# A hand-ordered attention and mixing kernel: q and k of the last batch transposed by DMA, less bias on TensorE, four loads in flight instead of six, and a new order

## The chip, the cores and the metric

The kernel runs on one core of a Trainium2 chip. The metric is the device time of one execution in microseconds (us). Every execution also gives the mean clock that was granted to TensorE, where 1.0 is full speed. One execution of each kernel was taken with the hardware profiler; the profile's span leaves out some 1.8 us of the device time.

## The reference

Four batches, eight heads, 768 positions and heads of 64. Attention comes first, over a window of 96 positions and 8 global ones. A mixer over tokens and channels follows, batch by batch.

```python
scores = scale * np.matmul(q, k.transpose(0, 1, 3, 2))
bias   = -slopes[:, None, None] * dist[None, :, :]
scores = np.where(keep, scores + bias, -1e9)      # keep: 8 global keys, or 0 <= rel < 96
a = softmax(scores)
x = np.matmul(a, v)                               # as (B, S, H*D)

theta = x @ w_theta
zr, zi = x * np.cos(theta), x * np.sin(theta)
u = x + w_tok_r @ zr + w_tok_i @ zi               # matrices of 768 x 768 over the tokens
out = u + np.maximum(u @ w_ch, 0.0)               # float32
```

## The kernel before

All work is cut into small named operations, and one long list, `ORDER`, fixes the order of the instructions on every engine. **Each engine takes its part of the list in that order**, and an instruction that waits holds what stands behind it: the changed kernel's VectorE, shown below, stood 4.84 us at one copy, with a normalise behind it whose matmuls had ended. The names that matter here are `t` (transposes of q or k), `q` and `k` (their evacuation from PSUM), `kp`/`kg` (a twin copy of transposed k), `bi` (bias matmuls), `s` (scores), `x` (exponential), `m` (multiply by a table), `vpa`/`vpb` (copies of the v tile, `vp<-vn`), `v` (the values matmul), `n` (normalise), `mx` (token mixing) and `ch` (channel mixing). The digits are batch, third of the sequence, pair of heads. `/DVE` and `/ACT` name the engine, and `+3` puts three filler matmuls on zeros ahead of an operation.

The constants, the loads with their gates, and the copies of v:

```python
    TQ = ()                 # thirds whose q and k are transposed by DMA
    DEPTH = 6               # loads in flight, batches 2 and 3
    DEPTH1 = 8              # batch 1
    BIASED = (0, 1, 2)      # thirds of batch 0 whose bias is added on TensorE
...
    def load(fn, us, ndesc, spot, depth=0, reads=(), writes=(), alloc=None):
        nload[0] += 1
        n = nload[0]
        landed[n] = spot
        ...
        if depth:           # the gate: a 1x1 copy out of the load `depth` before this one
            add(f"gate{n}", {"POOL": 0.35},
                lambda: nc.gpsimd.tensor_copy(out=scrap, in_=landed[n - depth]()), ...)
        add(f"load{n}", {"POOL": ...}, fn, ...)     # a DMA issued from GpSimd, with a cast to bf16
...
    for b in range(2, B):
        for g in range(G):
            batch(b, g, 0)   # four loads: q, q, k, k
            batch(b, g, 1)   # two loads: v, v        -> loads 47 to 82
...
    def vprev(b, g):
        def rest(o):         # vpa: the whole v tile
            vector[o.took](out=cut(dst), in_=cut(src))
        def head(o):         # vpb: its 8 global rows
            vector[o.took](out=cut(dst[0:NG]), in_=cut(src0[0:NG, 0:1]).to_broadcast([NG, 2, H, D + 1]))
```

A gate makes GpSimd wait until load n − DEPTH has landed, so at most DEPTH loads are in flight. The transposes and the scores:

```python
    def trans_qk(b, g, i, ts):
        if (b, g) in TQ:                     # by DMA, from SP's queue, SBUF to SBUF
            def go():
                ...
                nc.sync.dma_start_transpose(out=d_, in_=tiles[key][:, i].rearrange("n t c -> n (t c)"))
            ...
            return
        def pe():                            # on TensorE, then evacuated from PSUM
            for t in ts:
                for p in range(NP):
                    nc.tensor.transpose(p_[:, t - u0, p], tiles[key][:, i, t, p * T:(p + 1) * T], ident)
...
    def scores(b, g, p):
        biased = b == 0 and g in BIASED
        def bias(hh):                        # one matmul per head: slope * identity times distances
            nc.tensor.matmul(p_[:, 0:n], lhsT=sid[:, 2 * p + hh, :], rhs=dtab[:, s0:s0 + n], start=True, stop=False)
        ...
        if not biased:                       # or a multiply after the exponential, on VectorE
            def mul():
                nc.vector.tensor_mul(e_[:, :, 0:n], e_[:, :, 0:n], etab[:, 2 * p:2 * p + 2, s0:s0 + n])
```

The softmax here doesn't subtract the row's maximum and nothing guards it: scores larger than these inputs give would overflow.

Of the kernel before, what the change touches and what calls it, by code (L numbers as in the profile page):

```python
# [15 lines left out]
class Plan:  # L16
# [6 lines left out]
    def add(self, name, eng, fn, **_):  # L23
        op = self.ops[name] = SimpleNamespace(name=name, fn=fn, took=next(iter(eng)))
        return op
# [12 lines left out]
zero hw00 hw10 halfpi rel ones2 ones1 hw01 warm0 ones0 hw11 ones5 ones3 ones6 ones4 load1 tiny sid4 sid3 sid7  # L38
sid1 sid0 sid2 load2 sid5 sid6 ident far0 far1 load3 dtab0 dtab1 dtab2 load4 cast00/ACT dtab3 bi0000+1
cast10/DVE etab5 bi0001 t0000 load5 t0010 q000/ACT bi0010 bi0011 k000/DVE load6 etab7 kg000 cast01/DVE etab4  # L40
load7 kp000/DVE t0001+22 cast11/DVE etab1 s001 q001/DVE t0011 load8 etab0 s000 k001/DVE x0000 load9 kg001
x0001 kp001/DVE t0100+14 etab6 bi0020 load10 bi0021 q010/DVE x0010 t0110 x0011 s002 load11 k010/DVE etab2
bi0030 bi0031 s003 kp010/DVE x0020 load12 x0021 vpa00/DVE bi0100+2 x0030 kg010 vpb00/DVE bi0101+1 load13 x0031
s010 etab3 v000 v002 load14 v001 n000 x0100 bi0110 bi0111 vpa01/DVE s011 x0101 load15 vpb01/DVE bi0120 x0110
v003 n002 bi0121 load16 s012 x0111 n003 bi0130 load17 x0120 v010 n001 bi0131 s013 x0121 load18 n010 bi0200
x0130 v012 load19 v011 x0131 n012 t0200 gate20 t0210 n011 q020/ACT load20 v013 k020/DVE xt00 gate21 bi0201
kg020 xc00/ACT bi0210 kp020/DVE load21 bi0211 vpa02/DVE s020+1 n013 s021 gate22 x0200 vpb02/DVE load22 xt01+6
x0201 bi0220 x0210 xc01/DVE v020+1 bi0221 x0211 gate23 n020 bi0230 load23 s022 bi0231 x0220 s023 gate24 tw00
x0230 load24 th001 twc00/DVE x0231 gate25 x0221 v021 load25 v023 n021 ts0 tw10 gate26 v022 load26 twc10/DVE
th000 n023 gate27 tw11 n022 cos000 load27 th010 twc11/DVE sin000 xt02 gate28 cos001 z000 load28 tw01 sin001  # L50
th011 xc02/DVE gate29 cos010 z001 load29 th020 sin010 twc01/DVE gate30 cos011 load30 th021 z010 sin011 gate31
cos020 t1000 load31 z011 tw20 sin020 q100/DVE tw21 cos021 gate32 mx000 z020 load32 twc20/ACT twc21/DVE mx001
gate33 sin021 vpa10/DVE load33 tx1 vpb10/DVE t1010 z021 mx020 gate34 k100/DVE load34 mx002 kp100/DVE gate35
kg100 mx022 load35 u00 gate36 s100 load36 s101 ut00 x1000 mx021 gate37 x1010 uc00/DVE load37 x1001 tw31 x1011
u02 tw30 twc31/ACT gate38 s102 m100 load38 s103 t1100 x1020 m101 x1030 mx010 gate39 q110/DVE x1031 load39
x1021 v100 m103 mx012 twc30/ACT m102 gate40 load40 n100 tw40 v102 twc40/DVE mx011 gate41 n102 load41 t1110 u01
tw41 gate42 v103 k110/DVE load42 twc41/ACT ut01 ut02 v101 kg110 uc02/DVE ch00 uc01/ACT gate43 kp110/DVE load43
vpa11/DVE ch01 n103 gate44 load44 vpb11/DVE s110 n101 t1200 gate45 x1100 o00 load45 ch02 x1101 q120/DVE st00
t1210 gate46 o01 load46 s111 k120/DVE s112 st01 x1110 mx030 gate47 kp120/DVE x1120 load47 o02 mx032 x1121
kg120 gate48 x1111 m110 st02 mx031 load48 m111 s113 gate49 u03 s120 load49 x1130 tw50 m112 tw51 twc50/ACT v110  # L60
gate50 twc51/DVE xt10 load50 x1131 n110 mx040 vpa12/ACT xc10/DVE gate51 mx042 load51 m113 x1200 mx041
vpb12/DVE x1201 gate52 load52 m120 v111 mx050 n111 gate53 load53 u04 s121 v120 x1210 v113 gate54 n120 ut03
load54 x1211 mx052 n113 uc03/ACT gate55 m121 mx051 load55 vpa20/DVE s122 u05 gate56 s123 x1220 ch03 load56
vpb20/DVE x1221 ut04 x1230 gate57 o03 ut05 v121 load57 uc04/ACT v112 n121 th100 st03 uc05/ACT gate58 n112
x1231 load58 ch04 m122 ts1 m123 gate59 xt11 load59 v122 xc11/DVE cos100 v123 th101 gate60 n122 sin100 load60
n123 ch05 cos101 o04 gate61 sin101 xt12 load61 o05 st04 th110 xc12/ACT vpa21/DVE gate62 st05 z100 th111 load62
cos110 z101 sin110 th120 gate63 vpb21/DVE load63 cos111 z110 th121 sin111 gate64 cos120 load64 t2110 z111
sin120 t2010 k210/DVE gate65 cos121 t2200 load65 z120 mx100 k200/ACT kp210/DVE gate66 q220/DVE mx101 sin121
load66 kp200/DVE tx2 t2000 z121 gate67 mx120 kg210 load67 vpa22/DVE q200/DVE mx102 gate68 vpb22/DVE load68
kg200 mx110 u10 gate69 s200 load69 ut10 s201 mx111 x2000 x2001 gate70 x2010 mx121 load70 m200 x2011 v200 m201  # L70
gate71 mx112 load71 n200 s202 u11 gate72 s203 t2100 x2020 load72 x2021 mx122 ut11 q210/DVE x2030 gate73 x2031
m202 t2210 load73 u12 s210 k220/ACT s211 gate74 vpa30/DVE ut12 ch10 load74 vpb30/DVE x2100 kp220/DVE x2101
mx130 gate75 o10 load75 x2110 m210 s212 x2111 st10 mx131 gate76 m203 x2120 load76 m211 x2121 v210 mx132 n210
gate77 load77 m212 v201 s213 n201 ch11 gate78 x2130 load78 kg220 u13 x2131 v202 s220 n202 gate79 ut13 v203
load79 mx140 x2200 m213 x2201 n203 s221 gate80 load80 v212 vpa31/DVE x2210 xt20 mx142 m220 x2211 gate81 n212
s222 load81 v220 vpb31/DVE x2220 v213 n220 mx141 gate82 x2221 load82 n213 v211 m222 s223 ch12 n211 x2230 x2231
m221 v222 xt21 mx150 ts2 m223 v221 n222 v223 mx151 n221 n223 th200 o12 xt22 th201 o11 cos200 vpa32/DVE sin200
mx152 st11 u14 cos201 st12 vpb32/DVE ch13 sin201 ut14 u15 z200 th210 ut15 o13 th211 cos210 z201 sin210 st13
th221 cos211 z210 t3000 sin211 t3010 q300/DVE t3110 k300/DVE t3210 th220 k310/DVE k320/ACT kp300/DVE t3100
z211 cos220 mx200 kg300 q310/DVE sin220 mx201 cos221 kg310 kp310/DVE kg320 sin221 kp320/DVE t3200 z220 tx3  # L80
ch15 q320/DVE z221 s300 s301 mx220 x3000 o15 x3001 x3010 mx202 st15 m300 x3011 s302 m301 s303 mx222 u20 x3020
x3021 x3030 ut20 v300 m302 mx221 x3031 n300 v302 m303 ch14 n302 s310 o14 s311 x3100 mx210 u22 st14 x3110 v303
x3111 ut22 mx212 n303 x3101 m311 mx211 m310 v301 ch20 u21 n301 ut21 mx230 o20 s312 st20 s313 x3120 mx232 xt30
x3130 v310 x3121 ch22 n310 x3131 m312 s320 s321 o22 x3200 mx250 x3201 m313 st22 v311 x3210 mx231 n311 x3211
m320 s322 s323 u23 x3220 mx251 x3221 m321 ut23 v313 x3230 ch21 m322 x3231 n313 ts3 v312 v321 m323 mx240 n312
v320 o21 v322 xt31 mx241 n320 n321 v323 mx242 st21 n323 n322 th300 u24 xt32 mx252 cos300 sin300 th301 u25 ut24
z300 ch23 cos301 ut25 sin301 th310 o23 z301 th311 st23 cos310 sin310 mx300 cos311 z310 th320 sin311 z311 th321
cos320 sin320 mx301 cos321 z320 ch24 sin321 z321 mx310 o24 mx302 st24 mx311 u30 mx312 ut30 ch25 u31 mx320 ut31
o25 mx322 st25 mx321 ch30 u32 mx330 ut32 o30 mx331 st30 mx332 ch31 u33 mx340 ut33 o31 mx342 st31 mx341 ch32
u34 mx350 ut34 o32 mx351 st32 mx352 ch33 u35 ut35 o33 ch34 uc35/ACT st33 ch35 o34 ch351 o35 st34 o351 st35  # L90
st351
# [4 lines left out]
def kernel(  # L96
# [13 lines left out]
    nc = tc.nc  # L110
# [52 lines left out]
    TQ = ()  # L163
    TQ_AFTER = None
    DEPTH = 6
# [3 lines left out]
    BIASED = (0, 1, 2)  # L169
# [33 lines left out]
    add("dtab0", {"DVE": 0.34},  # L203
        lambda: nc.vector.tensor_tensor(dtab[:, 0:2], rel, far, op=ALU.add),
        reads=["far"], writes=["dtab"], prio=-6)
    add("dtab1", {"DVE": 0.11}, lambda: nc.vector.tensor_copy(out=dtab[:, 2], in_=dtab[:, 0]),
        reads=["dtab"], writes=["dtab"], prio=-6)
    add("dtab2", {"DVE": 0.14},
        lambda: nc.vector.tensor_scalar(dtab[0:NG, 0:2], dtab[0:NG, 0:2], float(NL), None, op0=ALU.min),
        reads=["dtab"], writes=["dtab"], prio=-6)  # L210
    add("dtab3", {"DVE": 0.14}, lambda: nc.vector.tensor_copy(out=dtab[:, 3:5], in_=dtab[:, 1:3]),
# [66 lines left out]
    def first(i, t):  # L278
# [18 lines left out]
        o = add(f"cast{i}{t}", {"DVE": 0.34, "ACT": 0.49}, cast, reads=[st], writes=[key, key + (i, t)],  # L297
# [77 lines left out]
    def twin(dst, mine, b, g, u0, n):  # L375
# [5 lines left out]

        def copy():
            d_ = tiles[dst][:, :, pr] if halves else tiles[dst][:, u0:u0 + n]
            vector[oc.took](out=d_[:, :, :, 1, NG:T], in_=d_[:, :, :, 0, NG:T])  # L384

        oc = add(f"kp{b}{g}{u0}", {"DVE": dve_t(512 * n, 4), "ACT": act_t(512 * n)}, copy, reads=mine, writes=[dst] + w2)
        add(f"kg{b}{g}{u0}", {"DVE": 0.1},
            lambda: nc.vector.tensor_copy(
                out=tiles[dst][:, td, kd, 1, 0:NG],
                in_=tiles["kk", b, 0][:, 0:1, kd, 0, 0:NG].to_broadcast([T, td.stop - td.start, kd.stop - kd.start, NG])),  # L390
            reads=mine + first_k, writes=[dst] + w2, boost=boost(b, 3))

    def trans_qk(b, g, i, ts):
# [404 lines left out]
```

## Time and profile before

| | before |
|---|---|
| median of 4 runs (range) | 171.19 us (170.99 to 171.66) |
| span of the profiled run | 169.6 us |
| TensorE busy | 162.1 us, 96% |
| VectorE busy | 136.0 us, 80% |
| load 47 issued, load 82 (the last) issued | 47.55 us, 86.22 us |

TensorE sets the time: it is never without work for long, and it runs at full clock. The prediction shows the lines for that. It does not show two lines on which the study turned. One concerns two v loads: the second of the two for the middle third of batch 3 (load 76), and the last load of all (load 82). The view is the timeline of GpSimd in the kernel before (start, us, engine, line, operation and tiles):

```profile
80.30 0.87 POOL L261 DMA_DIRECT2D vn<-in_v_dram  x1
...
86.22 0.93 POOL L261 DMA_DIRECT2D vn<-in_v_dram  x1
```

The other is the copy that needs load 76, in the timeline of VectorE of the same kernel:

```profile
94.05 0.43 DVE L457 COPY vp<-vn 128x1040 bf16<-128x1040 bf16 x1
```

Load 76 was issued at 80.30 us and landed about 5 us later. Its copy began at 94.05 us and waited for nothing. The load therefore had between 8 and 9 us to spare. From load 47 to load 82 one load was issued every (86.22 − 47.55)/35 = 1.105 us.

### The profile page before, as it was taken

Reading aid. Unit: us, or ns where it says so; the run is one execution under the profiler, and the core shown is the slowest. Engines: PE = TensorE matmul, PEld = TensorE weight load, DVE = VectorE, ACT = ScalarE, POOL = GpSimd, SP = SyncE. Lnnn points to the kernel's source line nnn. Section 1 sums busy time; section 2 is a strip of 40 time slices with the busy share of each in tenths; the row PEclk is TensorE's granted clock in tenths of the full one; section 3 lists DMA queues with packets and bytes.
Section 4 is the critical chain, followed back from the end, with each engine's and each line's share of the span. In section 5 each row is a group of like instructions: output and inputs, shape, how many; then the busy total and the mean of one; then the engine's idle time right before and its main releaser. Section 6 shows DMA issues by size and latency. Waiting matters only on the chain.

```text
span 169.6 us, 4122 instructions
## 1 busy us (share of the span) xinstructions
PE 162.1 (96%) x1581; PEld 91.9 (54%) x1608; DVE 136.0 (80%) x316; ACT 103.9 (61%) x186; POOL 80.7 (48%) x150
## 2 busy tenths in 40 slices
PE   7999999999999999999999999999999999999990
PEld 2665756656655656565555554754545644444440
DVE  7888987896999999998699999898859965634442
ACT  3799989986454939994695666695448557200010
POOL 8998689969989989999950000000000000000000
PEclk9999999999999999999999999999999999999999
DMA  4999999999999999999999438303363373143334
GB/s 134 208 155 155 197 191 177 190 178 178 162 164 197 197 143 137 164 221 141 135 156 139 93 66 216 93 0 97 93 126 98 74 173 97 62 108 108 95 97 182
DMA packets 94820, 23.73 MB, mean 140 GB/s; under 512 B 86992, under 2 KB 91856, under 8 KB 94800
## 3 DMA queue, kind: packets, MB, share of 16 engines
q0 software_dynamic: 73504, 12.33, 96.4%
q1 hardware_dynamic: 20240, 10.62, 23.4%
q10 hardware_dynamic: 1056, 0.52, 1.2%
q8 instruction: 12, 0.20, 0.5%
q14 instruction: 8, 0.07, 0.1%
HBM read 25.69 MB, written 6.29 MB: 189 GB/s over the span
## 4 chain that ended last, share of the span: by engine, by line
PE 87%; DVE 6%; ACT 2%; issue 2%; DVEq 0%
PE pb L644 37%; PE pa L601 12%; PE pb L688 10%; PE pa L499 7%; PE pb L425 5%; PE pa L556 5%; PE pa L490 3%; PE pb L367 2%; PE pb L582 2%; PE pb L556 2%; ACT e L526 1%; PE pb L668 1%; DVE sid L215 1%; ACT etab L742 1%; DVE kk L384 1%
## 5 line engine op out<-in xcount | busy, mean ns | idle before, releaser
L644 PE MATMUL pb<-zri,w_tokT 128*128 128x512 bf16 x273 | 67.6, 379 | 1.0 <-issue 0.3
L526 ACT ACTIVATE e<-pa 128x512 bf16<-128x512 f32 (+1 forms) x96 | 47.2, 568 | 25.1 <-PE pa L499 25.0
L644 PEld LDWEIGHTS <-w_tokT 128*128 128x128 bf16 x288 | 25.9, 98 | 26.7
L656 DVE TENSOR_TENSOR u<-x,pb 128x512 bf16<-128x512 bf16 x24 | 16.4, 683 | 11.1 <-PE pb L644 11.1
L534 DVE TENSOR_TENSOR e<-e,etab 128x1024 bf16<-128x1024 bf16 (+1 forms) x36 | 22.3, 639 | 2.6 <-ACT e L526 2.4
L688 PE MATMUL pb<-w_ch_bf,uT 128*128 128x512 bf16 (+1 forms) x96 | 24.0, 371 | 0.2
L601 PE MATMUL pa<-w_theta_bf,xT 128*128 128x512 bf16 x90 | 22.5, 379 | 0.3
L610 ACT ACTIVATE cs<-pa,halfpi 128x512 bf16<-128x512 f32 x24 | 16.8, 700 | 7.9 <-PE pa L601 7.8
L261 POOL DMA_DIRECT2D vn<-in_v_dram x24 | 21.2, 892 | 0.6 <-DMA qk<-in_q_dram 0.4
L247 POOL DMA_DIRECT2D qk<-in_q_dram x22 | 19.6, 890 | 1.4 <-issue 0.7
L247 POOL DMA_DIRECT2D qk<-in_k_dram x22 | 19.3, 879 | 0.4 <-issue 0.3
L622 DVE TENSOR_TENSOR zri<-x,cs 128x1024 bf16<-128x1024 bf16 x24 | 16.4, 685 | 3.5 <-ACT cs L612 3.5
L556 PEld LDWEIGHTS <-e 128*128 128x128 bf16 x352 | 15.0, 98 | 5.8
L694 DVE SCALAR_TENSOR_TENSOR o<-pb,u 128x512 f32<-128x512 f32 (+1 forms) x25 | 16.3, 663 | 2.3 <-PE pb L688 2.3
L569 DVE TENSOR_TENSOR x<-pa,rec 128x256 bf16<-128x256 f32 x36 | 15.3, 425 | 1.2
L499 PE MATMUL pa<-qT,kk 64*128 64x128 bf16 x352 | 15.9, 218 | 0.3 <-DVE qT L436 0.2
L499 PEld LDWEIGHTS <-kk 64*128 64x128 bf16 x352 | 10.0, 94 | 10.8 <-issue 8.1
L612 ACT ACTIVATE cs<-pa 128x512 bf16<-128x512 f32 x24 | 14.7, 612 | 0.0
L672 ACT COPY uT<-pb 128x512 bf16<-128x512 bf16 x5 | 2.8, 589 | 18.8 <-PE pb L668 18.8
L601 PEld LDWEIGHTS <-xT 128*128 128x128 bf16 x96 | 9.0, 98 | 9.5 <-DVE xT L585 0.2
L688 PEld LDWEIGHTS <-uT 128*128 128x128 bf16 x100 | 8.9, 98 | 8.8 <-ACT uT L672 0.5
L425 PE MATMUL pb<-ident,qk 128*128 128x128 bf16 x176 | 12.5, 219 | 0.1
(76 smaller groups left out, 205.3 us busy)
## 6 DMA issues: line engine op xcount, KB each, us to landing
out_dram<-o SPq DMA_DIRECT2D x23, 256.0 KB, 2.5
vn<-in_v_dram POOLq DMA_DIRECT2D x24, 128.0 KB, 5.6
qk<-in_q_dram POOLq DMA_DIRECT2D x22, 128.0 KB, 5.7
qk<-in_k_dram POOLq DMA_DIRECT2D x22, 128.0 KB, 5.5
w_nat<-in_moe_w_tok_r_dram POOLq DMA_DIRECT2D x6, 192.0 KB, 7.9
w_nat<-in_moe_w_tok_i_dram POOLq DMA_DIRECT2D x6, 192.0 KB, 7.3
e<-in_k_dram ACTq DMA_DIRECT2D x2, 256.0 KB, 5.0
e<-in_q_dram SPq DMA_DIRECT2D x2, 256.0 KB, 4.3
```

The lines of the kernel that those rows point to most:

```text
L247: nc.gpsimd.dma_start(out=tiles[key][:, i, t].rearrange("p (h d) -> p h d", d=D), in_=(q, k)[i][b, :, r0:r0 + T, :].rearrange("h p d -> p ...
L261: nc.gpsimd.dma_start(out=v_bufs[i][:, t, :, 0:D], in_=v[b, :, r0:r0 + T, :].rearrange("h p d -> p h d"))
L425: nc.tensor.transpose(p_[:, t - u0, p], tiles[key][:, i, t, p * T:(p + 1) * T], ident)
L499: nc.tensor.matmul(p_[hh][:, s], lhsT=tiles["kk", b, kg][R, kt, p, r, :], rhs=tiles["qT", b, g][R, qt, p, :], start=not biased, stop=not b ...
L526: nc.scalar.activation(tiles[ek][:, hh, 0:n], tiles[pb[hh]][:, 0:n], AF.Exp, scale=scale)
L534: nc.vector.tensor_mul(e_[:, :, 0:n], e_[:, :, 0:n], etab[:, 2 * p:2 * p + 2, s0:s0 + n])
L556: nc.tensor.matmul(o, lhsT=l_, rhs=r_, start=(i == 0), stop=(i == len(mms) - 1))
L601: nc.tensor.matmul(p_, lhsT=tiles["xT", b, g][:, p, t, :], rhs=w_theta_bf[:, p, :], start=(p == 0), stop=(p == NP - 1))
L610: nc.scalar.activation(tiles[ck][:, 0], tiles[ps], AF.Sin, bias=halfpi)
L622: nc.vector.tensor_mul(tiles[zk][:, t].rearrange("n i (p c) -> n i p c", p=NP), tiles["x", b, g][:, None, :, t, :].to_broadcast([T, 2, NP, ...
L644: nc.tensor.matmul(p_, lhsT=w_tokT[wi][:, 2 * g + t, tt * T:(tt + 1) * T], rhs=tiles["z", b, g][:, t, wi, :], start=(n == 1 and t == 0 and ...
L688: nc.tensor.matmul(p_, lhsT=tiles["uT", b, tt][:, p, :], rhs=w_ch_bf[:, p, i * w:(i + 1) * w], start=(p == 0), stop=(p == NP - 1))
```

## The change

The intent is to take matmuls off TensorE. The q and k of batch 3 are transposed by DMA, and the last third of batch 0 gets its bias from the table on VectorE. The loads are spread out by gates four deep, and a newly searched order fits it all together. The core of the diff, with the list cut:

```diff
-    TQ = ()
+    TQ = ((3, 0), (3, 1), (3, 2))
-    DEPTH = 6
+    DEPTH = 4
-    BIASED = (0, 1, 2)
+    BIASED = (0, 1)
 ORDER:
-... sid4 sid3 sid7 sid1 sid0 sid2 load2 sid5 sid6 ident far0 far1 load3 dtab0 dtab1 dtab2 ...
+... far0 far1 dtab0 load2 dtab1 dtab2 load3 dtab3 ident sid3 etab1 sid0 sid7 load4 ...
-... kg000 cast01/DVE etab4 load7 kp000/DVE t0001+22 ...
+... k000/ACT k001/DVE kp000/ACT kg000 load9 etab3 kp001/DVE s000+6 ...
-... load80 v212 vpa31/DVE x2210 xt20 mx142 m220 x2211 gate81 n212 s222 load81 v220 vpb31/DVE ...
+... ch11 vpa31/DVE load79 x2131 n211 mx140 vpb31/DVE gate80 m220 load80 v212 m213 s221 v220 ...
-... t3000 sin211 t3010 q300/DVE t3110 k300/DVE t3210 th220 k310/DVE k320/ACT kp300/DVE t3100 ...
+... n222 v223 t3000 mx151 ... t3010 ... t3110 ... t3100 ... t3210 ... kg300 kp300/DVE ... t3200 ...
```

The rest of the diff is the rest of the list and a few cost figures for the tool that searched the order; those change no instruction.

## The prediction

> **What bounds the kernel now.** I read the engines' busy shares first, then the chain of work that ended last, then single pieces of that chain for the price of each kind of matmul, then the queue that issues the DMA transposes, then loads.
>
> ```profile
> PE 162.1 (96%) x1581; PEld 91.9 (54%) x1608; DVE 136.0 (80%) x316; ACT 103.9 (61%) x186; POOL 80.7 (48%) x150
> PEclk9999999999999999999999999999999999999999
> PE 87%; DVE 6%; ACT 2%; issue 2%; DVEq 0%
> ```
>
> TensorE is busy 96% of the span, at full clock, and holds 87% of the chain; nothing else comes near. Busy time overlaps for pipelined matmuls, so I price the work from pieces of the chain where TensorE runs without a break (start, us, engine and tile, line, count):
>
> ```profile
> 107.16 1.79 PE pb L425 x32
> 160.29 2.59 PE pb L644 x12
> ```
>
> A 128-column transpose (L425) costs 1.79/32 = 0.056 us, a 512-column matmul (L644) 2.59/12 = 0.216 us. The program has 380,896 columns of matmul, counted from its instruction list; at 0.216/512 us per column that is 160.7 us. The last matmul starts at 165.5. So in 165.5 us there are only some 5 us in which TensorE does not stream: 1.2 before its first matmul, 1.7 because the eight warming matmuls run at half speed, and about 2 of true waiting. The waiting lies nearly all before 14 us:
>
> ```profile
> 4.58 0.53 PE L147 MATMUL pa<-zero 128*128 128x384 bf16 x1
> 4.58 0.15 PEld L490 LDWEIGHTS <-sid 128*128 128x128 bf16 x1 [0.27 <-issue]
> ...
> 5.27 0.62 DVE L211 COPY dtab<-dtab 128x256 bf16<-128x256 bf16 x1
> 5.29 0.79 PE L490 MATMUL pa<-dtab,sid 128*128 128x384 bf16 x2 [0.19 <-DVE dtab L209]
> ...
> 6.78 1.39 PE L145 MATMUL pb<-ident,zero 128*128 128x128 bf16 x22
> ```
>
> The bias matmuls wait for the table (dtab), which VectorE makes only after eight scaled identities (sid), and L145 is filler: transposes of zeros that the schedule puts where it expects TensorE to wait. Filler is waiting under another name; it must be counted with the work. From 14 us to 165.6 TensorE is saturated: what leaves its list there shortens the run, if nothing new makes it wait. After the last matmul come 4 us of output and end, untouched by the change.
>
> **What the skill says.** (1) The Trainium skill, "TensorE: Matmul & The Clock Gate", section "Wait — 56ns, not 53.3ns?": back-to-back matmuls start every N / 2.4 GHz plus about 2.5 ns when warm, 55.6 ns at 128 and 215.7 ns at 512 columns. The trace agrees (56 and 216), so every matmul removed is worth its columns plus a little. (2) "Perfetto Trace Analysis", section "Identifying the Most-Contended Engine": matmul busy share is no measure of closeness to the limit, because of pipelining. Hence my count by columns instead of by the 96%; here it leads to the same answer. (3) "DMA: Bandwidth & Descriptors", section "DMA Transpose (X-bar)": it takes 2-byte data, is issued from SP or ACT, lands in SBUF, and two issuing streams must not overlap. The data is bf16 and only SP issues transposes here, so it is legal and needs no evacuation from PSUM. No page gives its time at this size; the trace does:
>
> ```profile
> L589 SPq DMA_TRANSPOSE xT<-x x6: 1231/1236/1300, 94.2 to 136.5; - x6
> ...
> DMA to landing us min/median/max: 3.1/3.1/3.4
> ```
>
> The x transposes have the same shape as the new q and k ones (eight 128x128 blocks): 1.24 us of SP's queue each, 3.1 us to landing.
>
> **The change part by part.**
>
> *q and k of batch 3.* Removed from TensorE: 48 transposes x 0.056 = 2.7 us. They lie in the saturated stretch (107 to 112 us), so all of it counts. Removed with them: five VectorE copies of 0.69 us and one ScalarE copy of 1.03 us; neither engine ends the stage, so these are slack. Added: six transposes on SP, 6 x 1.24 = 7.4 us of queue time. SP's queue between 92 and 118 us shows what it must fit between:
>
> ```profile
> 94.16 8.38 SPq L589 DMA_TRANSPOSE xT<-x  x3
> 102.59 1.05 SPq L704 DMA_DIRECT2D out_dram<-o  x2
> 103.75 2.52 SPq L676 DMA_TRANSPOSE uT<-u  x2
> 106.37 8.35 SPq L704 DMA_DIRECT2D out_dram<-o  x2
> ```
>
> The 8.38 and 8.35 are mostly waits inside a row of issues. In the new order the first q transpose is issued before the last x transpose of batch 2, the first k after it and a u transpose. If that x transpose can go at about 101.5 us, the u follows to 104, k is issued till 105, lands at about 107, and its copy (0.41 us) is done by 107.5. The first scores of batch 3 start at 113.2 in the old run and should start near 110.5 in the new one. Estimated slack 3 us. The remaining four follow at 1.2 to 2 us each for groups needed 5 us apart.
>
> *Bias only on two thirds of batch 0.* Eight bias matmuls of 512 columns leave: 8 x 0.216 = 1.7 us. In their place four VectorE multiplies of 0.68 us (row L534) = 2.7 us on an engine that was 80% busy, and each now stands between exponential and values.
>
> *Filler.* Old: 42 of 128 columns, 1 of 384, 5 of 512, which is 42 x 0.056 + 0.16 + 5 x 0.216 = 3.6 us. New: 12 of 128, 12 of 384, 8 of 512, which is 0.7 + 1.9 + 1.7 = 4.3 us. The eight of 512 lie in the very third whose bias went: the schedule expects TensorE to wait for ScalarE and VectorE there, so the bias saves about nothing at its own place. Net +0.7.
>
> *New order at the start.* The table now comes before the identities (seven of them, 1.7 us in the row L215), so the first bias should not wait, and the exponential tables (0.74 us each on ScalarE) can begin near 4 instead of 5.9 us. ScalarE is 14.4 us busy of the 16 from 10 to 26 us, so it paces batch 0; it also loses one 1.0 us evacuation of x to VectorE. I expect 0.3 to 0.7 us of the 2 us of waiting to go. Doubtful, so I take 0.3.
>
> *Gates four deep instead of six,* for the loads of batches 2 and 3. They now land 4 to 6.5 us after issue and go out every 1.1 us, so four in flight allows one per about 1.2 us: over 36 loads the last slips from 86 to about 90 us. The k loads of the last third of batch 2 went out by 65.5 and had landed by 70, their transposes ran at 74 and later; batch 3 is wanted after 98. Worth zero.
>
> Sum on TensorE: -2.7 - 1.7 + 0.7 - 0.3 = -4.0 us. By columns alone it is 8,320 fewer, 3.5 us. From the larger figure I take back 0.3 us for small new waits from VectorE in batch 0: -3.7 us, 171.0 - 3.7 = 167.3 us.
>
> **Rivals.** (a) VectorE takes over in batch 0: multiplies, one more x copy and the value scaling fall into 18 to 31 us, nearly filling it (I add up some 12 us of rows for these 12 us). For: the 80%, and the strict order of its list. Against: spacing of its operations is shorter than their rows, and the filler shows that the schedule knows. It would take back 1 to 2 us: 168.5 to 169. (b) SP's queue becomes the wait in batch 3: a wait for one output holds all transposes behind it. For: the 8.35 us row of waiting. Against: 3 us of slack. If it holds the scores up by 2 us over the slack, TensorE idles as long: 169.5. (c) The loads, slowed by the gates, hold VectorE at a v copy or TensorE at a q transpose: the margin of 4 us speaks against it; 168 to 170. (d) The start gains more than I allow, the whole 2 us of waiting: 165.8.
>
> **Range and chances.** The sum is mostly subtraction on a saturated engine, so I trust it to about 1.2 us either way, with more room upwards since (a) to (c) only add: 166.0 to 169.0. A gain of 2% means below 167.6, only 0.3 above my figure: faster 0.56, same 0.42, slower 0.02.
>
> **What would show it.** Right: L425 with 128 instead of 176 transposes; DMA transposes of qT and kk at about 3.1 us to landing; no wait of scores or copies for them worth 0.3 us; the first bias without waiting for dtab; the last matmul at about 162; TensorE still near 96% busy. Wrong: waits of TensorE for VectorE in 18 to 31 us (a), for the k copy or a transposing DMA after 105 us (b), or of VectorE for vn between 60 and 95 us (c).

## The result

| | before | after |
|---|---|---|
| median of 4 runs | 171.19 us | 177.57 us |
| range | 170.99 to 171.66 | 175.40 to 177.95 |
| span of the profiled run | 169.6 us | 173.6 us |
| mean granted clock | 1.0 (profiled run) | 0.99 (profiled run), 0.977, 0.977, 0.981 |

The ratio is 1.0343, with a 95% interval of 1.0254 to 1.0431: slower by over 2%. A ratio here is the mean time of one kernel's fast runs over the mean of the other's in the same rounds, so it is not quite the ratio of the two medians (1.037). The profiled run of the changed kernel (175.40 us) was its fastest, so the profile shows less of the loss than most runs have.

The page of the changed kernel has these lines: busy time and share with instruction counts, the granted clock in 40 slices of 4.3 us, and the shares of the chain that ended last.

```profile
PE 160.6 (93%) x1513; PEld 88.6 (51%) x1536; DVE 134.8 (78%) x315; ACT 102.9 (59%) x185; POOL 82.1 (47%) x150
PEclk9999999999999999999999969999999999999999
PE 57%; DMA 21%; DVE 10%; issue 5%; POOL 2%; ACT 0%; DVEq 0%; POOLq 0%; ACTq 0%
```

TensorE's share of the chain fell from 87% to 57%, and DMA, which had none, holds 21%: from 49.58 to 96.78 us the chain consists of loads, and of GpSimd's gates and issues between them. One slice out of forty, at about 100 us, has a clock of 6 tenths. Both point to one place, and the chain of waits around it reads as follows (start, us, what):

```profile
90.02 6.76 DMA vn<-in_v_dram
...
96.87 0.44 DVE vp L456
...
97.43 0.43 DVE x L568
97.86 0.60 DVE vp L459
98.46 0.60 DVE e L533
...
99.11 0.42 PE pa L555 x8
```

A load of v is issued at 90.02 us and lands 6.76 us later. A copy on VectorE follows, then a normalise that it had held up, the second copy, then the multiply of e, and only then TensorE's values matmul. The same v load and the last load, in GpSimd's timeline:

```profile
90.02 0.87 POOL L260 DMA_DIRECT2D vn<-in_v_dram  x1
...
100.69 0.87 POOL L260 DMA_DIRECT2D vn<-in_v_dram  x1
```

Load 76 went out at 90.02 us instead of 80.30, and the last load at 100.69 instead of 86.22. Load 47 went out at 49.58 us, so one load took (100.69 − 49.58)/35 = 1.46 us instead of 1.105. VectorE's timeline shows what that does to the copy:

```profile
90.75 1.28 DVE L533 TENSOR_TENSOR e<-e,etab 128x1024 bf16<-128x1024 bf16 x2
96.87 0.44 DVE L456 COPY vp<-vn 128x1040 bf16<-128x1040 bf16 x1 [4.84 <-DMA vn<-in_v_dram]
```

VectorE had finished at 92.03 us and stood for 4.84 us before the copy. The brackets name the idle time and what ended it. The view of waits sums this up between 60 and 104 us (engine, tile and line, releaser, then us in total, times, longest):

```profile
POOL scrap L233 <- DMA qk<-in_q_dram: 4.9, 6, 1.2
...
DVE vp L456 <- DMA vn<-in_v_dram: 5.0, 2, 4.8
PE pa L555 <- DVE e L533: 4.3, 1, 4.3
```

GpSimd waits at its gates (`scrap` is a gate's target), VectorE for v, and TensorE for VectorE. The 4.3 us of TensorE are the first part of the loss. The second part stands in the windows of 2 us (stretch, length, busy us and count on TensorE, weight loads, VectorE, ScalarE and GpSimd, then granted clock, DMA share, GB/s):

```profile
96.00:98.00 2.00, 0.00 (x0) 0.00 (x0) 1.09 (x4) 0.00 (x0) 1.09 (x2) 1.00 2.41 155
98.00:100.00 2.00, 0.90 (x11) 0.53 (x12) 1.97 (x5) 0.00 (x0) 0.97 (x3) 0.91 2.76 141
100.00:102.00 2.00, 2.00 (x19) 0.97 (x19) 1.91 (x5) 0.44 (x1) 1.56 (x3) 0.50 0.82 48
102.00:104.00 2.00, 1.78 (x21) 0.81 (x20) 1.22 (x3) 0.79 (x3) 0.00 (x0) 0.74 1.65 117
```

TensorE does nothing from 96 to 98 us, and when work comes back its clock is halved. What full clock would have done and half clock did not is 2 us x (0.09 + 0.50 + 0.26) = 1.7 us. The Trainium skill, "TensorE: Matmul & The Clock Gate", section "What's actually happening", says that one idle window of about 3.4 us puts the clock back to half, and that about 3.4 us of busy time releases it. This trace agrees: TensorE stood idle for 4.30 us (from start to start, the gap in the record of matmuls is 4.47 us longer than its work), and 1.7 us lost at half clock are 3.4 us spent at it.

I laid the record of matmuls beside the instruction list and took, from the time between the first matmul's start and the last one's, the time that the columns in between need at the prediction's rate (0.216 us for 512). What remains, waiting or slow clock, is 3.8 us before and 11.1 us after; some 1.7 us of each is the half clock of the warming matmuls at the start.

In the unprofiled runs the mean clock is 0.977 to 0.981, lower than the 0.99 of the profiled one. The mean is taken over time and includes the end of a run, when TensorE has little or no work left (in b_tq's profile the clock is 0.91 over the last 4.9 us, of which TensorE is busy for 0.94), so it does not turn into lost time directly. The profiled run of b_tq (below) has a mean of 0.978 as well, and its trace shows 6.8 us at half clock. If the unprofiled runs of the changed kernel had as much, they lost at most 3.4 us to the clock, 1.7 us more than the profiled one; they are 1.9 to 2.6 us longer. This is an estimate from another kernel's trace, and not shown for these runs.

### The profile page after: what moved, and what is told of

Same layout as the page of the kernel before. It is cut to its first block, busy times and chain, and to the rows that moved or that the text cites.

```text
span 173.6 us, 3988 instructions
## 1 busy us (share of the span) xinstructions
PE 160.6 (93%) x1513; PEld 88.6 (51%) x1536; DVE 134.8 (78%) x315; ACT 102.9 (59%) x185; POOL 82.1 (47%) x150
## 4 chain that ended last, share of the span: by engine, by line
PE 57%; DMA 21%; DVE 10%; issue 5%; POOL 2%; ACT 0%; DVEq 0%; POOLq 0%; ACTq 0%
PE pb L643 25%; DMA qk<-in_q_dram 12%; PE pa L600 9%; PE pb L687 8%; DMA vn<-in_v_dram 7%; PE pa L498 4%; DMA qk<-in_k_dram 3%; PE pa L555 3%; PE pb L424 2%; PE pb L555 2%; PE pb L366 2%; POOL scrap L233 1%; DVE e L533 1%; DVE sid L214 1%; DVE vp L456 1%
## 5 line engine op out<-in xcount | busy, mean ns | idle before, releaser
L643 PEld LDWEIGHTS <-w_tokT 128*128 128x128 bf16 x288 | 26.5, 98 | 29.2 <-issue 1.1
L533 DVE TENSOR_TENSOR e<-e,etab 128x1024 bf16<-128x1024 bf16 (+1 forms) x40 | 24.8, 643 | 0.7 <-ACT e L525 0.5
L600 PE MATMUL pa<-w_theta_bf,xT 128*128 128x512 bf16 x94 | 23.3, 379 | 0.5 <-DVE xT L584 0.4
L498 PE MATMUL pa<-qT,kk 64*128 64x128 bf16 x352 | 16.5, 220 | 0.5 <-ACT kk L383 0.3
L555 PE MATMUL pa<-vp,e 128*128 128x65 bf16 x120 | 11.6, 195 | 4.4 <-DVE e L533 4.3
```

The costliest lines, as they stand in the source:

```text
L498: nc.tensor.matmul(p_[hh][:, s], lhsT=tiles["kk", b, kg][R, kt, p, r, :], rhs=tiles["qT", b, g][R, qt, p, :], start=not biased, stop=not b ...
L555: nc.tensor.matmul(o, lhsT=l_, rhs=r_, start=(i == 0), stop=(i == len(mms) - 1))
L600: nc.tensor.matmul(p_, lhsT=tiles["xT", b, g][:, p, t, :], rhs=w_theta_bf[:, p, :], start=(p == 0), stop=(p == NP - 1))
L643: nc.tensor.matmul(p_, lhsT=w_tokT[wi][:, 2 * g + t, tt * T:(tt + 1) * T], rhs=tiles["z", b, g][:, t, wi, :], start=(n == 1 and t == 0 and ...
```

## The experiments

The theory: four loads in flight cannot keep the old pace. The loads slide, VectorE stands at the copy of v, TensorE stands behind VectorE, and the idle time costs it its clock. The rivals: the DMA transposes, the bias on VectorE or the new start cost something of their own, or a late load hurts in another way. Fourteen kernels ran, and all outputs were correct. The times of the kernel before in the four groups of runs were 171.02, 171.01, 171.26 and 171.18 us (medians of 11 runs each), so differences between groups are uncertain by some 0.2 us.

| run | edit | median us (range, runs) | ratio to before [95%] |
|---|---|---|---|
| a_d6 | after, six in flight | 169.57 (168.95–169.66, 6) | 0.989 [0.987, 0.991] |
| b_d4 | before, four in flight | 173.55 (172.87–175.38, 4) | 1.015 [1.010, 1.020] |
| a_warm | after, filler at the wait | 180.51 (178.63–180.98, 4) | 1.052 [1.047, 1.057] |
| a_late | after, copies of v later | 172.85 (171.84–173.16, 4) | 1.010 [1.007, 1.013] |
| a_d8 | after, eight in flight | 169.95 (169.18–170.41, 6) | 0.992 [0.990, 0.995] |
| a_d6_pe | a_d6, transposes on TensorE | 173.42 (173.38–173.64, 4) | 1.013 [1.012, 1.015] |
| a_d6_bias | a_d6, all bias on TensorE | 170.41 (170.31–170.73, 6) | 0.996 [0.994, 0.997] |
| a_warm2 | after, filler placed earlier | 176.66 (174.49–178.44, 4, two of them slow) | 1.024 [1.020, 1.028] |
| b_tq | before, DMA transposes | 175.59 (174.91–176.68, 6) | 1.025 [1.023, 1.027] |
| a_d6_late | a_d6, copies of v later | 170.24 (169.27–170.51, 6) | 0.993 [0.990, 0.995] |
| a_d6_kp | a_d6, first twin copy on VectorE | 169.76 (169.11–170.27, 6) | 0.991 [0.988, 0.993] |
| a_d5 | after, five in flight | 169.26 (168.81–169.44, 4) | 0.988 [0.985, 0.990] |
| b_tq2 | b_tq, twin copies later | 169.07 (168.89–169.42, 6) | 0.987 [0.985, 0.989] |
| b_tq2_d5 | b_tq2, five in flight | 169.06 (168.75–169.37, 6) | 0.987 [0.985, 0.989] |

### a_d6: only the gates undone

```diff
-    DEPTH = 4
+    DEPTH = 6
```

> The changed kernel with the gates six deep again, all else kept. Theory (the late loads are the whole loss): loads go out every 1.1 us again, VectorE's 4.8 us wait for v is gone, clock 1.00, time 167.3 +-0.8 us. Rival (the DMA transposes or VectorE's multiplies have a cost of their own): 169.5 us or more.

The median was 169.57 us: 8.0 us less than the changed kernel, with a clock of 1.0. Pace, wait and clock came out as the theory had them, but the time lies above its band and just past the rival's mark of 169.5. The profiled span was 167.2 us. Load 76 in GpSimd's timeline of this run:

```profile
80.49 1.08 POOL L260 DMA_DIRECT2D vn<-in_v_dram  x1
```

And the copy in VectorE's:

```profile
91.46 0.43 DVE L456 COPY vp<-vn 128x1040 bf16<-128x1040 bf16 x1
```

The copy waits for nothing, 11 us after the load's issue. The loads go out every 1.122 us. Waiting of TensorE, worked out as above, is 4.7 us against 11.1, and the difference of 6.4 us is the difference of the two spans (173.6 − 167.2). The depth therefore explains the loss of the changed kernel. It does not explain why a_d6 is only 1.45 us faster than before, where the prediction had 3.7; the later runs go after that. This copy also begins 2.6 us earlier than in the kernel before (94.05), because the new order moved it.

### b_d4: the gates alone, on the old order

```diff
-    DEPTH = 6
+    DEPTH = 4
```

> The kernel before with the gates four deep, nothing else. Theory: its loads also go out every 1.45 us, the v copy of the middle third of batch 3 stands at about 94 us in VectorE's list and waits some 2 to 3 us, time 173 to 175 us. Rival (four deep only hurts in the new order): within 0.5 us of 171.2.

The median was 173.55 us, 2.5 us more than before. The loads went out every 1.456 us, as in the changed kernel, so the pace belongs to the depth and not to the order. VectorE's timeline shows the copies of the middle and the last third of batch 3:

```profile
95.67 0.74 DVE L457 COPY vp<-vn 128x1040 bf16<-128x1040 bf16 x1 [0.79 <-DMA vn<-in_v_dram]
...
106.91 0.44 DVE L457 COPY vp<-vn 128x1040 bf16<-128x1040 bf16 x1 [2.71 <-DMA vn<-in_v_dram]
```

The time lies in the expected band, though the wait at the middle copy was shorter than the 2 to 3 us expected. The same slide costs 0.79 and 2.71 us here where the changed kernel stood for 4.84, and the clock stayed at 1.0 in all four runs. For the middle copy, 2.85 us of the difference are its place: the new order brings VectorE to it at 92.03 us instead of 94.88. The other 1.2 us are a later landing (96.78 against 95.57), although load 76 was issued earlier there (90.02 against 91.78): it took 6.76 us to land in the changed kernel and 3.79 here. In the other profiled runs of the new order at four deep it took 6.0 to 8.2 us (a_warm2, a_warm, a_late), in a_d6 5.55. Why it lands slowly there is not shown. So the damage has three parts: the pace, the place of the copy, and the landing of this load.

### a_late: four in flight, but the copies later

```diff
-... ch11 vpa31/DVE ... mx140 vpb31/DVE ... vpa32/DVE ... vpb32/DVE ...
+... vpa31/DVE vpb31/DVE u20 ... vpa32/DVE vpb32/DVE n301 ...
```

> The changed kernel, gates still four deep, with the v copies of the middle and last third of batch 3 moved about 20 us later in VectorE's list. Theory (what hurts is a copy at the head of a strict list waiting for a late load): loads as late as in the changed kernel, no wait above 1 us, 168 to 169.5 us. Rival (the late loads starve something else as well): 171 us or more.

The median was 172.85 us: 4.7 of the 8.0 us came back with the loads as late as ever (the last at 101.80), and the clock was 1.0. The time is past the rival's mark of 171. The wait at the copy was thus the larger part of the loss, but not all of it: four deep instead of six costs 8.0 us with the early copies (177.57 against 169.57) and 2.6 us with the late ones (172.85 against 170.24 of a_d6_late). The waits of this run show a new one:

```profile
PE pa L600 <- DMA xT<-x: 1.3, 1, 1.3
```

The transposing DMAs of x landed after 4.4 us at the median and 9.0 at most, where they took 3.1 and 3.4 before. The Trainium skill, "DMA: Bandwidth & Descriptors", section "Issuing engines are not separate DMA queues", says that transfers of all issuing engines run on the same 16 engines and interleave. The trace fits that: loads that used to end at 86 us now run until after 101, beside the transposes. No run here separates that from a later start of the transposes' own inputs.

### a_warm and a_warm2: is the clock a cost of its own?

Filler was put where TensorE waits, so that it isn't idle while it waits.

```diff
 a_warm
-v220
+v220+18
 a_warm2
-s221
+s221+18
```

> The changed kernel with 18 filler matmuls of 512 columns (3.9 us) put where TensorE waits 4.5 us. Theory (part of the loss is TensorE's clock halved after the wait): the wait stays, the clock stays at 1.00, time about 173.5 us. Rival (the clock is a side show): 177 us or more, since the wait is as long as before.

This test failed, at 180.51 us. TensorE's timeline:

```profile
100.05 4.06 PE L146 MATMUL pa<-zero 128*128 128x512 bf16 x18 [3.18 <-DVE x L568]
```

The filler writes into a PSUM buffer that a normalise on VectorE has to free, and that normalise stands behind the same copy. So the filler waited too, and then added its 4.06 us. In a_warm2 it stands one operation earlier.

> The changed kernel, four deep, with 18 filler matmuls (3.9 us) one step earlier than in the run that missed: ahead of the scores before the wait, whose PSUM ScalarE frees. Theory (half clock after the wait costs the unprofiled runs about 4 us): VectorE still waits 4.8 us for v, the clock stays at 1.00, time 173 to 174.5 us. Rival (the clock costs little): 176.5 us or more.

Here the filler ran during the wait. The window from 96 to 100 us (columns as above):

```profile
96.00:100.00 4.00, 4.00 (x32) 1.82 (x31) 3.26 (x8) 0.09 (x1) 1.82 (x4) 1.00 2.15 121
```

TensorE is busy throughout and the clock is 1.00 in this window (0.998 over the run). The profiled run took 174.49 us, 0.9 less than that of the changed kernel, though it has 3.9 us more of filler. The two traces show where it gains: the values matmul behind the wait starts at 99.81 us, 0.7 later than the 99.11 of the changed kernel, and the last matmul at 168.52, 0.9 earlier than 169.38. These 1.6 us are made good by 103 us, where the changed kernel ran at half clock, and fit the 1.7 us worked out above. For this pair of runs the clock cost is shown. The times of all runs say less: two of the four count as slow, and of the two fast ones 174.49 us lies inside the theory's band (173 to 174.5) and 175.97 between it and the rival (176.5 or more). How much the clock makes of the 8 us in a typical run stays an estimate.

### a_d8, a_d5 and a_d6_late: is there a best depth?

```diff
 a_d8, a_d5 (on the changed kernel)
-    DEPTH = 4
+    DEPTH = 8, or 5
 a_d6_late: DEPTH = 6, and the copies of v as in a_late
```

> The changed kernel with gates eight deep. Theory (at six deep the loads are already paced by the time POOL needs to issue them, 1.12 us each): as six deep, 169.6 +-0.4 us. Rival (six deep still holds some loads back, in the executions of 169.6 more than in those of 169.0): 169.0 us or less.

Eight in flight gave 169.95 us, as expected, and no better than six. Waits between 80 and 90 us:

```profile
PE pb L687 <- DMA uT<-u: 1.0, 1, 1.0
```

A transposing DMA of u, 2.5 us at the median, took up to 6.9 us. That this comes from the greater depth is not shown: the longest took 5.9 us at six deep (a_d6) and 7.7 at five (a_d5).

> The changed kernel, gates five deep. If the loads' pace is the latency over the depth (6 us over 5 = 1.2 us), the last load goes out at about 91 us instead of 87 and 101, the v copy waits well under 1 us, and the time is 169.5 to 170.5 us. If four is a cliff for another reason than pace: 173 us or more.

Five gave 169.26 us, 0.2 below the expected band. The last load was issued at 90.73 us, as expected, and no copy on VectorE waited for v. The edge thus lies between four and five, and there is nothing to gain on the other side: 169.26, 169.57 and 169.95 for five, six and eight.

> The changed kernel, six deep, with the v copies of the last two thirds of batch 3 later in VectorE's list. Theory (in most executions six deep still loses 0.6 us at these copies): 169.0 us or less. Rival (the copies no longer wait for anything at six deep): within 0.3 us of six deep alone, 169.6.

With six in flight, later copies gained nothing (170.24 us, 0.7 more than a_d6 and so outside both forecasts; TensorE waited 0.8 us for a transposing DMA of u). The early place of the copies is harmful only with four.

### a_d6_pe and a_d6_bias: the other two parts, undone one at a time

```diff
 a_d6_pe (on a_d6)
-    TQ = ((3, 0), (3, 1), (3, 2))
+    TQ = ()
+    ... z201 t3000 t3010 q300/DVE t3110 k300/DVE t3210 k310/DVE k320/ACT mx200 ...
+    ... th221 t3100 q310/DVE t3200 q320/DVE ...
 a_d6_bias (on a_d6)
-    BIASED = (0, 1)
+    BIASED = (0, 1, 2)
+    bi02p0 bi02p1 ahead of each s02p; m020 to m023 out; the 8 filler matmuls of this third out
```

> The changed kernel, six deep, with q and k of batch 3 transposed on TensorE again (48 transposes, five copies on VectorE and one on ScalarE back). Theory (TensorE is saturated there, each transpose costs its 0.056 us): 2.7 us more than six deep alone, 172.0 to 172.6 us. Rival (the stretch has slack, or the DMA transposes bring waits of their own): 171 us or less.

The run took 173.42 us, 3.85 us more than a_d6. The 48 transposes are 2.7 us. The rest is of my making: I put two evacuations of q ahead of the z products on VectorE, and TensorE waited there (its timeline):

```profile
113.68 0.59 PE L643 MATMUL pb<-zri,w_tokT 128*128 128x512 bf16 x2 [1.10 <-DVE zri L621]
```

The DMA transposes are worth at most 3.85 us and, less that wait, some 2.7. The time is above the theory's band (172.0 to 172.6) by 0.8 us.

> The changed kernel, six deep, with the last third of batch 0 biased on TensorE again: eight bias matmuls for the eight fillers of that third, the four multiplies on VectorE gone. Theory (the bias matmuls gave way to filler, so nothing was gained there): within 0.4 us of six deep alone, 169.2 to 170.0 us. Rival 1 (the table way saves TensorE 1.7 us): 171 us or more. Rival 2 (VectorE's multiplies hold batch 0 up): 168.8 us or less.

The run took 170.41 us, 0.84 us slower than a_d6, outside the band that I gave. Its columns are the same as those of a_d6, because eight bias matmuls of 512 columns took the place of eight filler matmuls of 512. TensorE's waiting between 20 and 30 us rose by only about 0.3 us; the larger new waits came later, 0.74 us near 72 us for a copy of xT and 0.6 us near 87 us for a DMA of uT. So leaving the bias out does not hurt, but I can't name what it gains.

### a_d6_kp: the start

```diff
-k000/ACT k001/DVE kp000/ACT
+k000/ACT kp000/DVE k001/DVE
```

> The changed kernel, six deep, with the first copy of k's twin on VectorE again, ahead of the second k evacuation. In the changed order it stands on ScalarE, waits there for VectorE and lets the first exponential start at 10.8 us, 0.8 later than before. Theory (ScalarE paces batch 0, so its start counts): first exponential at about 9.9 us and 0.4 to 0.9 us less than six deep alone, 168.7 to 169.2. Rival (the fillers and TensorE's fixed order take it up): 169.6 as six deep alone.

In the changed kernel the first exponential starts at 10.79 us, later than before (10.01). Just ahead of it in ScalarE's timeline stands a twin copy that waited for VectorE:

```profile
9.65 0.59 ACT L383 COPY kk<-kk 128x480 bf16<-128x480 bf16 x1 [0.59 <-DVE kk L435]
```

With that copy on VectorE the time was 169.76 us, no gain over 169.57, as the rival had it.

### b_tq, b_tq2 and b_tq2_d5: the DMA transposes alone, on the old order

```diff
 b_tq (on before)
-    TQ = ()
+    TQ = ((3, 0), (3, 1), (3, 2))
     q3xx and k3xx out; the six t3xxx placed among SP's other issues
 b_tq2 (on b_tq): twin copies after their transposes
+    ... kp300/DVE kg300 tx3 ... kg310 kp310/DVE x3001 ... kg320 kp320/DVE x3101 ...
 b_tq2_d5 (on b_tq2)
-    DEPTH = 6
+    DEPTH = 5
```

> The kernel before (its order, six deep, three thirds biased) with nothing but q and k of batch 3 transposed by DMA. Theory (48 transposes at 0.056 us leave a saturated TensorE, and the rest of the changed kernel's smaller gain is the new order's waits): 168.3 +-0.5 us. Rival (the DMA transposes pay only within the new order): 169.8 us or more.

It missed: 175.59 us. I had left the twin copies where they stood, ahead of the landing of k. VectorE's timeline, and then TensorE's:

```profile
115.80 0.41 DVE L383 COPY kk<-kk 128x960 bf16<-128x960 bf16 x1 [3.30 <-DMA kk<-qk]
```

```profile
116.86 1.44 PE L643 MATMUL pb<-zri,w_tokT 128*128 128x512 bf16 x3 [3.46 <-DVE zri L621]
```

It is the fault of the changed kernel in another place. A copy at the head of VectorE's list waits for a DMA, TensorE waits 3.46 us behind it, and the mean clock of the run is 0.978. The windows after the gap (columns as above) show the half clock:

```profile
116.00:118.00 2.00, 1.14 (x3) 0.41 (x3) 2.00 (x5) 0.00 (x0) 0.00 (x0) 0.51 0.11 21
118.00:120.00 2.00, 2.00 (x16) 0.84 (x15) 1.54 (x4) 0.80 (x3) 0.00 (x0) 0.50 0.34 131
120.00:122.00 2.00, 2.00 (x12) 0.93 (x10) 0.86 (x3) 0.83 (x3) 0.00 (x0) 0.50 0.32 66
122.00:124.00 2.00, 2.00 (x14) 0.77 (x12) 1.36 (x4) 0.00 (x0) 0.00 (x0) 0.79 0.00 0
```

That is 2 us x (0.49 + 0.50 + 0.50 + 0.21) = 3.4 us below full clock, so 6.8 us at half clock after a gap of 3.46 us, twice as long as in the changed kernel after 4.30 us. The profiled run of a_warm idled for 3.18 us and kept a clock of 1.0.

> The kernel before with q and k of batch 3 transposed by DMA, as in the run that missed, with the three twin copies of k moved later in VectorE's list. Theory (48 transposes at 0.056 us leave a saturated TensorE; the new order brings waits of its own): no wait of VectorE for kk above 0.5 us, clock 1.00, 168.3 +-0.6 us, below every variant of the changed kernel. Rival (the new order is needed to harvest the transposes): 169.5 us or more.

With the twin copies moved behind their transposes the same kernel took 169.07 us, 2.1 less than before, 0.2 above the expected band and below the rival. The span was 167.4 us. The issue of the first k transpose, from SP's timeline:

```profile
105.75 1.23 SPq L401 DMA_TRANSPOSE kk<-qk  x1
```

And the first scores of batch 3, from TensorE's:

```profile
110.59 0.51 PE L498 MATMUL pa<-qT,kk 64*128 64x128 bf16 x12
```

The scores wait for nothing. TensorE's waiting is 4.0 us against 3.8 before, and the last matmul starts at 163.15 us instead of 165.53: 2.4 us earlier, for 6,144 columns that are worth 6,144 x 0.216/512 = 2.6.

> As b_tq2, gates five deep. Theory (five deep paces the loads at 1.2 us, late by 4 us at the end, which costs nothing, and lets the transposes of u land sooner): within 0.4 us of b_tq2. Rival (five deep already holds the v copies of the old order up): 169.5 us or more.

Five in flight on top of that gave 169.06 us, the same. These two have the lowest medians, 1.3% below the kernel before and 4.8% below the changed one. But a_d5, the changed kernel with one figure altered, is only 0.2 us above them, which is within the uncertainty between groups.

## Why the prediction was wrong

The prediction was 167.3 us with a range of 166.0 to 169.0; the result was 177.57. Step by step:

**The gates are the step that failed.** The prediction had: "four in flight allows one per about 1.2 us: over 36 loads the last slips from 86 to about 90 us", and "Worth zero". The measured pace was 1.46 us, in both orders, and the last load slipped to 100.69. One round of four took 4 x 1.46 = 5.8 us, where the working assumed some 4.8 (1.2 x 4); its own range of landings, 4 to 6.5 us, would have allowed 1.0 to 1.6 us per load. Read load by load in the changed kernel's trace, a load landed 4.97 us after its issue on average (3.4 to 7.7 us), and the load that this landing let go was issued another 0.84 us later. Of this, 0.57 us passed even where GpSimd already stood at the gate: the gate's own copy and the hand-over. The rest are landings that came while GpSimd was busy with earlier loads. So the landing was nearly as assumed, and the missing term is the time at the gate. Load 47 itself also went out 2.0 us late, after a gate that waited 1.86 us for a load of weights. In all, GpSimd waited 12.1 us for loads at its gates between 46 and 102 us. With six in flight it hardly waited there (not at all in the kernel before, 1.1 us in a_d6), because six issues at 1.105 us are 6.6 us, longer than most landings: the pace was that of GpSimd's own issues and gates.

**The margin was read at the wrong consumer.** The prediction checked the k loads of batch 2 and took batch 3 to be "wanted after 98". The copies of v for batch 3 stand in VectorE's list long before TensorE needs them: at 94.05 us before, and at 91.46 in the new order (a_d6). At the predicted pace load 76 would have gone out at 49.58 + 29 x 1.2 = 84.4 us and landed in time; at 1.46 it did not. The landing of this load then took 6.76 us, against 5.04 in the kernel before. Rival (c) named exactly this wait, "hold VectorE at a v copy", but was dismissed with "the margin of 4 us", and its 168 to 170 us did not count what a gap of over 4 us does to TensorE's clock. Its sign, "waits ... of VectorE for vn between 60 and 95 us (c)", is what came: VectorE stood from 92.03 to 96.87 us.

**Transposes by DMA: right.** The prediction had −2.7 us, and b_tq2 gives −2.1 in time and −2.4 at the last matmul. A landing of 3.1 us was expected; a_d6 shows 3.1 to 3.7. The first k transpose goes out at 103.54 us in a_d6 (about 105 allowed), and the first scores of batch 3 begin at 111.32 (110.5 predicted). SP's queue, rival (b), held nothing up.

**Filler and bias: the columns were right, what they brought was not.** The program has 8,320 columns fewer, as counted. But a_d6, with the loads in order, starts its last matmul at 162.96 us: 2.6 us earlier and not 3.5, because its waiting is 0.9 us more (4.7 against 3.8). The "−1.7" of the bias was to be cancelled by filler in its third. Undoing it costs 0.84 us in a_d6_bias, so it is worth something. Yet a_d6 (169.57) and a_d5 (169.26) are no faster than b_tq2 (169.07), which has the old order, but for the transposes and twin copies, and all the bias. By difference, the new order seems to cost about as much as the smaller bias saves; no run tested the new order alone.

**The start: wrong in sign, and small.** A gain of 0.3 us was expected. The table was indeed ready, and of the first bias matmuls in the changed kernel's timeline of TensorE, one waits 0.27 us for an identity instead:

```profile
4.53 0.34 PE L489 MATMUL pa<-dtab,sid 128*128 128x384 bf16 x1
...
6.00 0.34 PE L489 MATMUL pa<-dtab,sid 128*128 128x384 bf16 x1 [0.27 <-DVE sid L214]
```

In the first 20 us the waiting of a_d6 is 4.4 us against 4.2 before, and the first exponential is 0.8 us later.

**VectorE in batch 0, rival (a): not seen.** Between 20 and 30 us TensorE waited 0.1 us or less, before as after.

What stays open: in which waits the new order loses its 0.9 us of columns. They are spread over small ones between 60 and 110 us, and most runs of a_d6 are 0.6 us slower than the one that was profiled. Open too is the exact share of the clock in the typical loss of 8.0 us.

## What to carry to other kernels

A limit on transfers in flight is a pace: the landing time plus the time at the gate, over the depth (5.8/4 us here), or the issuing engine's own time per transfer where that is longer (1.1 us here, at six). It has to be held against the first instruction that reads the data on any engine, with the lists as they are after the change. A copy that seems to have slack is on the critical path as soon as it stands at the head of a strict list, because everything behind it waits as well; when a new order comes with a new depth, look for the readers that moved forward. A gap on TensorE can cost more than itself: here 4.30 us of it were followed by 3.4 us at half clock and 3.46 us by 6.8, while after 3.18 us the clock stayed full.

## What the Trainium skill lacked or had wrong

- "DMA: Bandwidth & Descriptors", section "Anatomy of one DMA — SWDGE (gpsimd) path": its fit (2.0 us plus the bytes over 436 GB/s) would make 2.3 us of a load of 128 KB in bf16 (2.6 of its 256 KB in float32). The loads here, which cast and are cut into rows of 64 values, landed after 3.9 to 6.8 us in the kernel before (median 5.0). The page says elsewhere that small descriptors are slow, but has no time for a load like these.
- No page has what a limit on loads in flight does to their pace: 1.105 us per load at six, and 1.46 at four, for landings of about 5 us.
- "DMA: Bandwidth & Descriptors", section "DMA Transpose (X-bar)", has no time at this size; the page gives an effective bandwidth of DMA transposes elsewhere, but no time to landing for one. Eight blocks of 128x128 in bf16 took about 1.25 us of SP's queue and landed after 3.1 us, and after up to 9.0 us beside late loads (a_late).
- "TensorE: Matmul & The Clock Gate" does not say how long the half clock lasts after one gap of a given length: 3.4 us after 4.30 us idle (the changed kernel), 6.8 us after 3.46 (b_tq), none after 3.18 (a_warm). The mean clock of one program was 0.99 in one run and 0.977 to 0.981 in three others.
